# Loading the second FFN weight in two halves behind the first key transfers

## The chip, the cores and the metric

The kernel runs on one core of a Trainium2 chip. The core has five engines, each of which works through its own list of instructions in order: PE (TensorE, matrix products into PSUM banks; its weight loads are shown apart, as PEld), DVE (VectorE), ACT (ScalarE), POOL (GpSimd) and SP (SyncE). Here SP does nothing but issue DMA transfers. They all go into one queue, which 16 DMA engines work off. An instruction can wait for a semaphore that another engine, or a landed transfer, has raised. While it waits, everything behind it on its own engine waits too. The metric is the device time of one execution in microseconds (us). The figure for the kernel before is the median of three runs.

## The reference

A transformer block with attention and a gated feed-forward network (FFN) side by side, both fed from the same normalized input:

```
xn = layernorm(x)                       # x: 1 x 2048 x 512, bf16
q, k, v = split(xn @ wqkv)              # 32 heads of 16
p = softmax(q @ k.T * 16 ** -0.5)       # per head, 2048 x 2048
attn = (p @ v) @ wo
h = silu(xn @ w1) * (xn @ w3)           # 2048 x 1792
out = x + attn + h @ w2                 # w2: 1792 x 512
```

## The kernel before

**Scheduling.** The Python code of `_build` does not write the engines' lists out by hand. It keeps queues of work items (`miscq`, `expq`, `redq`, `poolq`, `spq` and others) and in a loop (L2034) takes, over all engines, the item that could start first by its own model of durations. So the order on each engine is fixed when the program is built. The item goes to the end of its engine's list together with the waits that its data need. Transfers enter `spq` through `later_dma`; an item with a `pred` is a candidate only once that function returns true. Among the candidates `pick_sp` (L2015) takes the one that could start earliest. On the chip SP then issues strictly in the order so found. Each transfer raises one of 24 semaphores, used in rotation.

**Start.** The input x and the weight wqkv are loaded (L596, L600), then two tiles of x again and the first pieces of w1 and w3 (L996, L624, L626), and two DRAM buffers are filled with constants (L614, L617). x is normalized in 16 tiles of 128 rows. PE transposes each (L771), and ACT copies the transposed tile t out as `xnT` tile t (L778); the name ("xnT", t) then enters the set `done`.

**Keys and queries.** Heads go in groups of four, and within a group each head takes a 32-row strip of the partitions. For the first group PE writes keys and queries straight into that layout. For the others ACT copies a product into `kq` (L857), a transfer spreads it into a DRAM buffer (kd or qd, L828), and a second one fetches it back as `KT` or `QT` in the strip layout (L845, L850). The first such key transfers are the pair KT<-kd at 21.14 us in the trace.

**Attention.** Work goes by units: one group of heads and 256 query rows (a few units have 128). In a first pass PE computes all scores of a unit (L1166) and DVE takes the maximum of each row (L1205). The negated maxima go into spare rows of `QT`: for the first units through PE and ACT (L922), for the others through a transposing transfer `Zs<-Z` (L1353) and two copies `QT<-Zs` (L1349). In a second pass PE computes the scores again, transposed and with the maximum taken off, and ACT takes the exponential into `PT` (L1479, or L1509 over two banks). PE then multiplies `PT` by the values `Vaug` (L673).

**Masked queries.** The second pass has two forms for a block of scores. One uses the 32-row strip of a single head (L1454). The other uses all 128 rows of `KT` against `BD`, which holds the unit's queries with the strips of the other three heads at zero (L669). `bd_prep` puts four transfers `BD<-QT` on `spq` for each unit, one for each head (L1291). Each copies 32 rows, for a unit of 128 query rows 8 KB in all. Where the built program uses `BD`, PE's matmul waits for that transfer.

**FFN and output.** w1 and w3 come in pieces of 128 columns, 128 KB each, as the work proceeds (L624, L626). `w2` is loaded once. `wo` is cleared by POOL (L652), and when that has been put on POOL's list, `late_loads` puts the four transfers of `wo` (L657, 128 KB each, into 16 of the 128 partitions) and the one of `w2` (L659, 1,792 KB, all 128 partitions, rows of 1 KB) on `spq`. The transfer of `w2` has no `pred` and waits for no data. `g_h` is the matmul that reads `w2`; it first runs at 349.3 us.

Of the kernel before, what the change touches and what calls it, by code (L numbers as in the profile page):

```python
# [254 lines left out]
def _c_mm(n):  # L255
    return n / 2400.0 + (0.007 if n >= 512 else 0.004)
# [6 lines left out]
def _build(nc, A_x, A_wqkv, A_wo, B_w1, B_w3, B_w2, out):  # L263
# [5 lines left out]
    FC = F // 128  # L269
# [40 lines left out]
    BD_END = 4  # L310
    NORM = "dddppppp"
    STATS = "dddddaaa"
    R_STAT = 2
    R_SEC = 1
    SPLIT_LO = 20
# [137 lines left out]
    def sb(name, shape, dt):  # L453
        return ctx.enter_context(nc.sbuf_tensor(name, list(shape), dt))

    with ctx:
# [7 lines left out]
        xnT = sb("xnT", [128, DC, S], BF16)  # L464
        hT = sb("hT", [128, NHT, 512], BF16)
# [14 lines left out]
        w2 = sb("w2", [128, FC, D], BF16)  # L480
# [46 lines left out]
        w2_v = B_w2.rearrange("(c p) n -> p c n", p=128)  # L527
# [19 lines left out]
        done = set()  # L547
# [12 lines left out]
        def later_dma(fn, reads, writes, lat=2.3, cb=None, pred=None, occ=0.62):  # L560
            spq.append(_Item(fn, reads, writes, occ, lat, cb, pred))
# [50 lines left out]
        def prefill():  # L612
            for b_ in range(2):
                later_dma(lambda e, b_=b_: e.dma_start(  # L614
                    kd[b_][:, 16:32, :], ones_t[:, :].unsqueeze(1).broadcast_to([128, 4, 128])),
                    [("ones_t",)], [("kd", b_)], lat=4.0, cb=lambda op, b_=b_: kd_free["K"].append(b_))
                later_dma(lambda e, b_=b_: e.dma_start(qd[b_][:, 16:32, :], Z[:, :, :, :]),  # L617
                          [("Z", 0), ("Z", 1)], [("qd", b_)], lat=4.0,
                          cb=lambda op, b_=b_: kd_free["Q"].append(b_))

        def load_w13(idx):
            fc = idx % FC
            sl = idx % 3
            later_dma(lambda e: e.dma_start(w13[:, sl, 0:DC, :], w1_v[:, :, fc * 128:(fc + 1) * 128]),  # L624
                      [], [("w13", sl, 0)])
            later_dma(lambda e: e.dma_start(w13[:, sl, DC:2 * DC, :], w3_v[:, :, fc * 128:(fc + 1) * 128]),  # L626
                      [], [("w13", sl, 1)], cb=lambda op: done.add(("w13", idx)))
# [13 lines left out]
        for g in padq:  # L641
# [7 lines left out]
                                  pred=lambda: ("AUG", 0) in done))  # L649
        poolq["pad"].append(_Item(lambda e: e.memset(Vaug[:, :, :, 16:17], 1.0), [],  # L650
                                  [("Vone",)], 2.4, pred=lambda: ("AUG", 0) in done))
        poolq["pad"].append(_Item(lambda e: e.memset(wo[:, :, :], 0.0), [], [("wo",)], 3.5,  # L652
                                  cb=lambda op: late_loads(), pred=lambda: ("AUG", 1) in done))

        def late_loads():
            for j in range(4):
                later_dma(lambda e, j=j: e.dma_start(wo[32 * j:32 * j + 16, :, :], wo_v[j]), [("wo",)],  # L657
                          [("wor", j)])
            later_dma(lambda e: e.dma_start(w2[:, :, :], w2_v), [], [("w2",)], lat=12.0)  # L659


        def col_groups(bk, make_lhsT, rhs_ap, ncols, c0=0, start=True, stop=True, m=32, skip=False, n=4, own=False):
            full = n == 4 and m == 32 and not own

            def part(a, b, start, skip):
                def f(e):
                    kw = dict(skip_group_check=True) if skip else {}
                    if full:
                        return e.matmul(bank(bk)[:, c0 + a:c0 + b], make_lhsT(0, 128), rhs_ap(0)[:, a:b],  # L669
                                        start=start, stop=stop, **kw)  # L670
                    for i in range(n):
                        rhs = rhs_ap(i)
                        ins = e.matmul(bank(bk)[32 * i:32 * i + m, c0 + a:c0 + b], make_lhsT(i),  # L673
                                       rhs if (a, b) == (0, ncols) else rhs[:, a:b],
                                       start=start, stop=stop, tile_position=(0, 32 * i), **kw)
                    return ins
                f.full = full
                return f
            f = part(0, ncols, start, skip or ncols == 512)
            if ncols == 512:  # L680
                f.piece = lambda a, b: part(a, b, start and a == 0, True)
                f.at = 0
            return f
# [3 lines left out]
        def ln_chunk(gi):  # L687
# [4 lines left out]
            left = [t1 - t0]  # L692
            on_act = STATS[gi] == "a"
            if on_act:
# [234 lines left out]
        def hslot(idx):  # L929
            return (idx + DC) % NHT  # L930
# [73 lines left out]
        def g_h(tg, fc, stop=False):  # L1004
            qc, ts = divmod(tg, 4)
            hs = hslot(qc * FC + fc)
            return (lambda bk: col_groups(bk, lambda i, z=32: hT[:, hs, ts * 128 + 32 * i:ts * 128 + 32 * i + z],
                                          lambda i: w2[:, fc, :], D, start=False, stop=stop),
                    [("hT", hs), ("w2",)], _c_mm(512), None)

        def g_on(qc, ts, g, start, stop):
            ob = (qc + 1) % 2
# [9 lines left out]
        def tile_OUT(tg):  # L1022
            qc, ts = divmod(tg, 4)
            groups = [g_x(tg)] + [g_h(tg, fc) for fc in range(FC)]
            groups += [g_on(qc, ts, g, False, g == NG - 1) for g in range(NG)]

            def evac(bk):
                def cb(op):
                    store(tg)
                    done.add(("OUT", tg))  # L1030
                    if tg + NXR < NT:
                        load_xr(tg + NXR)
                return [_Item(lambda e: e.activation(osb[:, tg % 4, :], bank(bk), ACTF.Identity),
                              [("ps", bk)], [("osb", tg % 4)], _c_act(512), cb=cb)]
            return _Tile("OUT%d" % tg, groups, evac, pred=lambda: ("xr", tg) in done
                         and (tg < 4 or ("ST", tg - 4) in done)
                         and all(("hT", qc * FC + fc) in done for fc in range(FC))
                         and all(("ON", qc, g, ts) in done for g in range(NG)), paced=True)
# [4 lines left out]
        def tile_OUTA(tg):  # L1043
            qc, ts = divmod(tg, 4)
            groups = [g_x(tg)] + [g_h(tg, fc, NGA == 0 and fc == FC - 1) for fc in range(FC)]
            groups += [g_on(qc, ts, g, False, g == NGA - 1) for g in range(NGA)]

            def evac(bk):
                def cb(op):
                    done.add(("OUTA", tg))  # L1050
                    if tg + NXR < NT:
                        load_xr(tg + NXR)
                if to_dve():
                    return [_Item(lambda e: e.tensor_scalar(opart[ts], bank(bk), 1.0, 0.0, ALU.mult, ALU.add),
                                  [("ps", bk)], OP_KEYS[ts], _c_dve(512), cb=cb, name="dve")]
                return [_Item(lambda e: e.activation(opart[ts], bank(bk), ACTF.Identity),
                              [("ps", bk)], OP_KEYS[ts], _c_act(512), cb=cb)]
            return _Tile("OUTA%d" % tg, groups, evac, pred=lambda: ("xr", tg) in done
                         and all(("hT", qc * FC + fc) in done for fc in range(FC))
                         and all(("ON", qc, g, ts) in done for g in range(NGA)))  # L1060
# [869 lines left out]
        def cand(eng, it, dma=False):  # L1930
            return max(P.free[eng], P.ready(eng, it.reads, it.writes, dma))
# [13 lines left out]
        def pick_act():  # L1945
# [13 lines left out]
            for k, it in enumerate(miscq[:14]):  # L1959
                if okp(it):  # L1960
                    s = cand("act", it)
                    r = {"first": 0, "second": R_SEC, "stat": R_STAT}.get(it.name, 2)
                    if m is None or s < m[0] - 1e-6 or (s < m[0] + 1e-6 and r < m[2]):
# [65 lines left out]
        load_w13(0)  # L2029
        load_w13(1)  # L2030
        prefill()

        seg = [0]
        while True:  # L2034
# [49 lines left out]
def bass_parallel_sum__mha_block__glu_gated_swiglu__prompt_kernel(  # L2084
    nc: bass.Bass,
    A_x: bass.AP,
    A_wqkv: bass.AP,
    A_wo: bass.AP,
    B_x: bass.AP,
    B_w1: bass.AP,  # L2090
    B_w3: bass.AP,
    B_w2: bass.AP,
    out: bass.AP,
):
    _build(nc, A_x, A_wqkv, A_wo, B_w1, B_w3, B_w2, out)
# [28 lines left out]
```

## Time and profile before

| | us |
|---|---|
| median of three runs | 1195.73 |
| the three runs | 1195.73, 1195.26, 1197.73 |
| the profiled execution | 1194.81 |
| its span, first to last instruction | 1193.1 |
| DVE busy in it | 1167.4 |
| ACT busy in it | 1164.2 |
| PE busy in it | 1113.7 |
| POOL busy in it | 460.7 |
| mean granted clock of PE | 0.995 of full speed |

The profile is of one execution. A row of the timeline gives the start, the duration, the engine, the source line, the operation, what it writes and reads (out<-in), how many were merged, and in brackets the idle time before it with what ended it. SPq rows are the issues of transfers on SP, not the transfers themselves. Buffer numbers are left out of names, so `w` stands for `w2` and for the pieces of w1 and w3 alike; the line tells them apart. A row "A <- B: total, times, longest" of the waits says that A sat idle until B was done. The chain follows the last instruction back through what released it at each step.

### The profile page before, as it was taken

Reading aid. Unit: us, or ns where it says so; the run is one execution under the profiler, and the core shown is the slowest. Engines: PE = TensorE matmul, PEld = TensorE weight load, DVE = VectorE, ACT = ScalarE, POOL = GpSimd, SP = SyncE. Lnnn points to the kernel's source line nnn. Section 1 sums busy time; section 2 is a strip of 40 time slices with the busy share of each in tenths; the row PEclk is TensorE's granted clock in tenths of the full one; section 3 lists DMA queues with packets and bytes.
Section 4 is the critical chain, followed back from the end, with each engine's and each line's share of the span. In section 5 each row is a group of like instructions: output and inputs, shape, how many; then the busy total and the mean of one; then the engine's idle time right before and its main releaser. Section 6 shows DMA issues by size and latency. Waiting matters only on the chain.

```text
span 1193.1 us, 36078 instructions
## 1 busy us (share of the span) xinstructions
PE 1113.7 (93%) x14891; PEld 527.2 (44%) x15026; DVE 1167.4 (98%) x1083; ACT 1164.2 (98%) x2259; POOL 460.7 (39%) x925
## 2 busy tenths in 40 slices
PE   8799999989999999999989999999999999989998
PEld 4344444334444443444434443444434444345654
DVE  8799999999999999999999999999999999999995
ACT  7699999999999999999999999999999999999998
POOL 5334473334433236343342135534342125533320
PEclk9899999999999999999999999999999999999999
DMA  5412323211101112211111112111110112101100
GB/s 181 125 47 71 92 55 80 58 40 45 42 22 40 42 45 53 51 31 36 32 39 29 43 44 63 40 41 33 44 27 22 42 33 62 28 23 22 25 20 23
DMA packets 144040, 56.34 MB, mean 47 GB/s; under 512 B 105996, under 2 KB 143876, under 8 KB 143876
## 3 DMA queue, kind: packets, MB, share of 16 engines
q1 hardware_dynamic: 143876, 54.02, 17.8%
q8 instruction: 119, 1.95, 0.7%
q14 instruction: 45, 0.37, 0.1%
HBM read 38.67 MB, written 6.74 MB: 38 GB/s over the span
## 4 chain that ended last, share of the span: by engine, by line
ACT 66%; PE 20%; DVE 12%; issue 1%; DMA 1%; POOL 0%; ACTq 0%; SPq 0%; POOLq 0%
ACT PT L1479 46%; DVE part L1205 11%; ACT PT L1509 10%; PE ps L669 8%; PE ps L673 4%; PE ps L1454 4%; PE ps L1166 4%; ACT zg L968 2%; ACT th L962 2%; ACT ub L972 2%; ACT U L1573 1%; DMA BD<-QT 1%; ACT kq L857 1%; ACT RB L1273 1%; PE ps L1815 1%
## 5 line engine op out<-in xcount | busy, mean ns | idle before, releaser
L1205 DVE TENSOR_REDUCE part<-ps 128x2 f32<-128x1024 f32 x1004 | 1138.4, 1211 | 8.4 <-PE ps L1454 7.4
L1479 ACT ACTIVATE PT<-ps 128x512 bf16<-128x512 f32 x1720 | 928.5, 750 | 8.8 <-PE ps L669 6.3
L1454 PE MATMUL ps<-QT,KT 32*128 32x256 bf16 (+1 forms) x3322 | 447.8, 257 | 10.4 <-ACT PT L1509 1.5
L1166 PE MATMUL ps<-KT,QT 32*128 32x512 bf16 x2066 | 419.4, 384 | 11.6 <-DVE part L1205 7.6
L1454 PEld LDWEIGHTS ps<-QT,KT 32*128 32x128 bf16 x3322 | 157.3, 92 | 159.0 <-ACT PT L1479 79.1
L673 PE MATMUL ps<-PT,Vaug 128*17 128x256 bf16 (+1 forms) x4672 | 205.0, 261 | 2.3 <-ACT PT L1479 0.2
L1509 ACT ACTIVATE PT<-ps 128x1024 bf16<-128x1024 f32 x164 | 187.8, 1177 | 0.7 <-PE ps L1454 0.6
L1166 PEld LDWEIGHTS ps<-KT,QT 32*128 32x128 bf16 x2066 | 102.8, 91 | 159.6 <-DVE part L1205 86.5
L1598 POOL TENSOR_TENSOR Rc<-Lc,mone 128x8 f32<-128x8 f32 (+1 forms) x69 | 105.0, 1522 | 158.2 <-DMA Lc<-U 157.9
L669 PE MATMUL ps<-xnT,w 128*128 128x512 bf16 (+3 forms) x606 | 151.7, 313 | 13.1 <-ACT PT L1479 4.2
L669 PE MATMUL ps<-BD,KT 128*128 128x256 bf16 (+1 forms) x834 | 147.4, 266 | 13.8 <-DMA BD<-QT 6.2
L673 PEld LDWEIGHTS ps<-PT,Vaug 128*17 128x17 bf16 x4672 | 91.7, 90 | 77.9 <-issue 56.4
L673 PE MATMUL ps<-BD,KT 128*32 128x256 bf16 (+1 forms) x2064 | 93.6, 265 | 0.3 <-ACT kq L857 0.2
L669 PEld LDWEIGHTS ps<-BD,KT 128*128 128x128 bf16 x834 | 64.8, 98 | 50.3 <-ACT PT L1479 11.1
L669 PEld LDWEIGHTS ps<-xnT,w 128*128 128x128 bf16 x647 | 50.4, 97 | 76.7 <-issue 36.6
L669 PE MATMUL ps<-w,hT 128*128 128x512 bf16 (+3 forms) x332 | 78.1, 304 | 4.1 <-ACT U L1573 2.6
L1330 POOL TENSOR_TENSOR mx<-part 128x16 f32<-128x16 f32 (+1 forms) x67 | 14.1, 211 | 169.3 <-DVE part L1205 169.0
L669 PE MATMUL ps<-xnT,ident 128*128 128x512 bf16 (+3 forms) x238 | 67.3, 318 | 12.4 <-DVE part L1205 4.9
L951 POOL TENSOR_TENSOR hT<-a,t 128x512 bf16<-128x512 f32 x56 | 71.0, 1268 | 2.9
L949 POOL TENSOR_TENSOR a<-zg,ub 128x512 f32<-128x512 bf16 x56 | 64.6, 1153 | 19.5 <-ACT ub L972 19.5
L1618 POOL TENSOR_TENSOR wk_on<-U,R 128x256 bf16<-128x256 f32 (+1 forms) x36 | 22.9, 636 | 119.6 <-DMA R<-rd 119.5
L947 POOL TENSOR_SCALAR t<-th 128x512 f32<-128x512 bf16 x56 | 34.7, 620 | 85.8 <-ACT th L962 84.9
(110 smaller groups left out, 746.9 us busy)
## 6 DMA issues: line engine op xcount, KB each, us to landing
w<-in_B_w_dram SPq DMA_DIRECT2D x112, 128.0 KB
R<-rd SPq DMA_DIRECT2D x55, 128.0 KB
QT<-qd SPq DMA_DIRECT2D x31, 128.0 KB
KT<-kd SPq DMA_DIRECT2D x28, 128.0 KB
BD<-QT SPq DMA_DIRECT2D x220, 16.0 KB
PT<-in_A_x_dram SPq DMA_DIRECT2D x4, 512.0 KB
xr<-in_A_x_dram SPq DMA_DIRECT2D x16, 128.0 KB
out_dram<-osb SPq DMA_DIRECT2D x16, 128.0 KB
```

The lines of the kernel that those rows point to most:

```text
L669: return e.matmul(bank(bk)[:, c0 + a:c0 + b], make_lhsT(0, 128), rhs_ap(0)[:, a:b], start=start, stop=stop, **kw)
L673: ins = e.matmul(bank(bk)[32 * i:32 * i + m, c0 + a:c0 + b], make_lhsT(i), rhs if (a, b) == (0, ncols) else rhs[:, a:b], start=start, stop ...
L947: q.append(_Item(lambda e: e.tensor_scalar(t1[:, :], th[:, ss, :], 1.0, 1.0, ALU.mult, ALU.add), [("th", ss)], [("t1",)], 0.62, 0.72))
L949: q.append(_Item(lambda e: e.tensor_tensor(a32[:, :], zg[:, ss, :], ub[:, ss, :], ALU.mult), [("zg", ss), ("ub", ss)], [("a32",)], 1.1, 1.25))
L951: q.append(_Item(lambda e: e.tensor_tensor(hT[:, hslot(idx), :], a32[:, :], t1[:, :], ALU.mult), [("a32",), ("t1",)], [("hT", hslot(idx))] ...
L962: lazyq.append(_Item(lambda e: e.activation(th[:, ss, :], zg[:, ss, :], ACTF.Tanh), [("zg", ss)], [("th", ss)], 0.52, cb=part_done))
L1166: ins = e.matmul(bank(2 * sl + i), QT[32 * j:32 * j + 32, qs, q * 128:(q + 1) * 128], KT[32 * j:32 * j + 32, g, c_ * 512:(c_ + 1) * 512], ...
L1205: redq.append(_Item(lambda e: e.tensor_reduce(dst, pair_ap.rearrange("p (a b) -> p a b", b=512), AX.X, ALU.max), writes, [("part", par, qt ...
L1454: ins = e.matmul(bank(b)[:, i * nq:(i + 1) * nq], KT[32 * j:32 * j + 32, g, (k0 + i) * 128:(k0 + i + 1) * 128], QT[32 * j:32 * j + 32, qs, ...
L1479: expq.append(_Item(lambda e: e.activation(PT[:, sl, :], bank(b), ACTF.Exp, scale=SCALE), [("ps", b)], [("PT", sl)], _c_act(512), cb=cb, e ...
L1509: return _Item(lambda e: e.activation(PT[:, s0:s1 + 1:s1 - s0, :], ps8[:, b0:b1 + 1:b1 - b0, :], ACTF.Exp, scale=SCALE), [("ps", b0), ("ps ...
L1598: poolq["nrm"].append(_Item(lambda e: e.tensor_tensor(Rc[:, pp, 0:nl], Lc[:, pp, 0:nl], mone[:, 0:nl], ALU.pow), [("Lc", pp), ("mone",)], ...
```

## The change

The transfer of `w2` leaves `late_loads`. In its place two transfers, of 7 of the 14 row blocks each, are put on `spq` right after the initial loads. Each may be taken once the scheduler has placed the copy of `xnT` tile 8, and each waits for that copy on the chip as well. `w2` now has two names, ("w2", 0) and ("w2", 1), and every matmul of `g_h` depends on both.

```
+    W2_AT = 8
...
             for j in range(4):
                 later_dma(lambda e, j=j: e.dma_start(wo[32 * j:32 * j + 16, :, :], wo_v[j]), [("wo",)],
                           [("wor", j)])
-            later_dma(lambda e: e.dma_start(w2[:, :, :], w2_v), [], [("w2",)], lat=12.0)
...
-                    [("hT", hs), ("w2",)], _c_mm(512), None)
+                    [("hT", hs), ("w2", 0), ("w2", 1)], _c_mm(512), None)
...
         prefill()
+        for i in range(0, FC, FC // 2):
+            later_dma(lambda e, i=i: e.dma_start(w2[:, i:i + FC // 2, :], w2_v[:, i:i + FC // 2, :]), [("xnT", W2_AT)],
+                      [("w2", i // (FC // 2))], lat=6.0, pred=lambda: ("xnT", W2_AT) in done)
```

In the built program the two halves stand on SP between the first KT<-kd pair and the qd<-kq that follows it, where before they stood, as one, between a kd<-kq and the second group of BD<-QT issues:

```
before                              after
KT<-kd x2                           KT<-kd x2
                                    w2<-B_w2 (7 of 14) x2
qd<-kq                              qd<-kq
QT<-qd x2                           QT<-qd x2
kd<-kq                              kd<-kq
KT<-kd x2                           KT<-kd x2
BD<-QT x4                           BD<-QT x4
kd<-kq                              kd<-kq
w2<-B_w2 (14 of 14)
BD<-QT x2                           BD<-QT x2
KT<-kd x2                           KT<-kd x2
BD<-QT x2                           BD<-QT x2
wo<-A_wo x4                         wo<-A_wo x4
```

The rest of SP's list, and the lists of PE, DVE, ACT and POOL, hold the same instructions in the same order. Some waits name another semaphore of the rotation, and four matmuls gain or lose a wait for a transfer that the other version has covered by an earlier one.

## The prediction

> **What bounds the kernel now.** I read the page's first part, then the busy time by stage, then the waits, the chain and the DMA queue of the one stage that falls out of line.
>
> ```profile
> span 1193.1 us, 36078 instructions
> PE 1113.7 (93%) x14891; PEld 527.2 (44%) x15026; DVE 1167.4 (98%) x1083; ACT 1164.2 (98%) x2259; POOL 460.7 (39%) x925
> ```
>
> DVE and ACT are both busy 98% of the span, so there are only some 26 and 29 us of idle time in which anything could be won without removing work. The busy time by stage says where they lie (columns: stretch, its length, busy us of PE, PEld, DVE, ACT, POOL, granted clock, DMA share, GB/s):
>
> ```profile
> 41.00:51.00 10.00, 9.50 (x111) 5.32 (x111) 9.94 (x11) 10.00 (x22) 6.56 (x6) 1.00 0.35 98
> 51.00:57.30 6.30, 0.08 (x1) 0.01 (x1) 1.12 (x1) 0.61 (x2) 1.65 (x8) 0.60 1.12 280
> 57.30:66.00 8.70, 8.05 (x72) 3.65 (x75) 6.40 (x6) 6.99 (x11) 0.00 (x0) 0.70 0.19 21
> 66.00:100.00 34.00, 33.07 (x488) 15.36 (x490) 34.00 (x31) 34.00 (x69) 13.82 (x27) 1.00 0.25 62
> 100.00:600.00 500.00, 470.27 (x5916) 213.09 (x5971) 499.71 (x446) 498.29 (x962) 207.59 (x381) 1.00 0.20 49
> 600.00:1100.00 500.00, 470.71 (x6274) 218.46 (x6325) 500.00 (x449) 498.80 (x971) 190.36 (x395) 1.00 0.15 37
> ```
>
> From 66 to 1100 us DVE is idle for 0.29 us in all and ACT for 2.9 us. Nothing is to be won there, and whatever moves the start of that stretch moves its end by as much. The hole is 51 to 66 us: in these 15 us DVE works 1.12 + 6.40 = 7.52 us and ACT 0.61 + 6.99 = 7.60 us, which leaves 7.48 and 7.40 us idle. The longest waits between 40 and 70 us say on what:
>
> ```profile
> DVE part L1205 <- PE ps L1454: 7.2, 3, 6.6
> ACT PT L1479 <- PE ps L669: 6.3, 1, 6.3
> PE ps L669 <- DMA BD<-QT: 6.2, 1, 6.2
> ```
>
> DVE and ACT wait for PE, and PE for one transfer, a masked-query copy BD<-QT. The chain in order of time gives that copy's life:
>
> ```profile
> 47.70 0.34 SPq L1291
> 48.05 0.04 issue
> 48.09 9.09 DMA BD<-QT
> 57.18 0.14 issue
> 57.32 0.80 PE ps L669 x5
> ```
>
> It is an 8 KB copy, and it took 9.09 us. The DMA queue's own rows say what stood ahead of it (start, length of the issue, line, out<-in, count):
>
> ```profile
> 21.14 0.82 SPq L845 DMA_DIRECT2D KT<-kd  x2
> 28.57 0.60 SPq L828 DMA_DIRECT2D qd<-kq  x1
> 31.45 0.80 SPq L850 DMA_DIRECT2D QT<-qd  x2
> ...
> 41.70 2.52 SPq L1291 DMA_DIRECT2D BD<-QT  x4
> 46.08 0.64 SPq L828 DMA_DIRECT2D kd<-kq  x1
> 46.76 0.45 SPq L659 DMA_DIRECT2D w<-in_B_w_dram  x1
> 47.31 1.71 SPq L1291 DMA_DIRECT2D BD<-QT  x2
> 49.22 0.90 SPq L845 DMA_DIRECT2D KT<-kd  x2
> 50.16 1.15 SPq L1291 DMA_DIRECT2D BD<-QT  x2
> 51.36 2.83 SPq L657 DMA_DIRECT2D wo<-in_A_wo_dram  x4
> 54.23 1.30 SPq L1353 DMA_TRANSPOSE Zs<-Z  x1
> 64.35 0.66 SPq L828 DMA_DIRECT2D kd<-kq  x1
> 65.06 1.13 SPq L1349 DMA_DIRECT2D QT<-Zs  x2
> ```
>
> The w<-in_B_w_dram at 46.76 is w2, all 1,792 KB of it, issued 0.55 us before the two copies on which PE then stops. So the stall is one small transfer behind one large one.
>
> **The change part by part.** In the order of instructions, PE, DVE, ACT and POOL run exactly what they ran before, in the same order; only SP's list differs.
>
> *w2 removed from 46.76.* PE stopped at 57.32 - 6.24 = 51.08 us. How late will the copy be without w2? Its two issues took 1.71 us, against 2.52 / 4 = 0.63 us each for the four at 41.70. They start at 47.3 in either case, since the first waits for ACT. So they end between 48.6 and 49.0. The nearest row for the landing of a transfer with nothing ahead of it is qd<-kq: its issue ends at 29.17, and what waits for it goes out at 31.45, 2.3 us later. BD then lands at 50.9 to 51.3, against 51.08 when PE wants it: a wait of 0 to 0.2 us. A copy of 8 KB should land sooner than one of 128 KB, so I take 0 and keep 0.3 us for the range. What goes with the wait is the slow clock behind it. The clock column gives its edges: 0.60 over 6.3 us means full speed up to 52.3, half after; 0.70 over the next 8.7 us means half speed until 62.5. So PE ran at half speed for 5.2 us after it had its data, and ACT's idle time beyond its 6.3 us wait, 7.40 - 6.3 = 1.1 us, is the price of that. With no pause neither occurs. Off this comes what a stretch of that length idles anyway: 0.06 us in ten before it for DVE, none for ACT. Both engines gain 7.4 us, and both are full up to 1100 us, so the end moves by 7.4 us less at most 0.3.
>
> *w2 put behind the first KT pair, in two halves.* The first half waits for ACT's copy of the ninth transposed tile, the L778 row that starts at 21.68:
>
> ```profile
> 21.68 0.63 ACT L778 ACTIVATE xnT<-ps 128x512 bf16<-128x512 bf16 x1
> ```
>
> It ends at 22.31, after the KT issues (21.14 + 0.82 = 21.96). SP's next instruction, qd<-kq, does not go out before 28.57, because it waits for ACT. So two issues of 0.45 us (w2's own row) fit, and nothing on SP stands behind the new wait. What the queue carries there (same columns as above):
>
> ```profile
> 3.00:13.00 10.00, 10.00 (x85) 7.59 (x82) 8.19 (x24) 3.65 (x10) 2.96 (x7) 1.00 1.09 371
> ...
> 24.00:29.00 5.00, 4.72 (x36) 1.94 (x35) 5.00 (x6) 5.00 (x15) 3.07 (x8) 1.00 0.00 0
> ...
> 55.00:58.00 3.00, 0.68 (x5) 0.46 (x5) 0.00 (x0) 0.06 (x1) 0.00 (x0) 0.50 1.15 121
> 58.00:60.00 2.00, 1.67 (x18) 0.83 (x18) 1.23 (x1) 1.95 (x3) 0.00 (x0) 0.50 0.34 39
> 60.00:62.00 2.00, 2.00 (x17) 0.61 (x14) 1.50 (x2) 1.35 (x3) 0.00 (x0) 0.50 0.00 1
> ```
>
> From 24 to 29 us it moves nothing. At the 371 GB/s of the opening loads, 1.835 MB take 4.9 us; at the slowest pace of a full queue in these rows, 121 GB/s, 15.2 us. The same kind of load (many rows of 1 KB over all partitions) gave the 371, so I take 4.9 us from the end of the two issues, 22.3 + 0.9 = 23.2: done at 28.1, at 30.4 with the 2.3 us of a landing, so qd<-kq is late by 0 to 1 us. The cover is in SP's waits:
>
> ```profile
> SPq L217 <- ACT QT L922: 5.2, 1, 5.2
> ```
>
> That is the first BD<-QT at 41.70, which stands behind qd, QT, kd and KT on SP and waited 5.2 us for ACT. Up to 5.2 us of delay reaches no engine. Cost taken: 0.
>
> *What is late next.* With BD on time, PE goes on through its list to the first scores that read the rows from Zs:
>
> ```profile
> 68.40 0.28 PE L1454 MATMUL ps<-QT,KT 32*128 32x256 bf16 x1
> ```
>
> That is 11.08 us after 57.32, of which 1.1 us was slow clock, so about 51.1 + 10.0 = 61.1 us. Their rows need the Zs transposition (54.23), and it stands behind wo. In the 121 GB/s of 55 to 58 us I read wo, 512 KB into 16 partitions a piece: 4.3 us at that pace, from about 52.4, so Zs lands near 57.5. QT<-Zs stands behind kd on SP, which follows ACT: 64.35 was 7.0 us after 57.32, so it comes at 51.1 + 5.9 = 57.0, and QT<-Zs at 57.7. Slack about zero in front of the issue, and then 65.06 to 68.40, 3.3 us from issue to use, of which some 2 are transfer. Cost 0, at worst the second rival below.
>
> *Sum.* The profiled execution took 1194.81 us around a span of 1193.1; 1194.81 - 7.4 = 1187.4. Its time lies 0.92 us under the median of the runs, 1195.73; on the median the forecast is **1188.3 us**. Its own range is 1187.2 to 1189.3: the 0.3 us above, 0.1 us more gain from DVE, and the rest for a median that scatters about 0.7 us.
>
> **The rivals.** *Zs takes the place of BD.* If wo is as slow without w2 beside it, the queue empties at 60 as it does now (39 GB/s up to 60, 1 after). Then QT<-Zs goes out at 60.0 to 61.1 and lands some 2 us later, 1 to 2 us after 61.1; say 1.5. The half clock came 1.2 us after PE had stopped (52.3 against 51.08), so it may come again and cost its 1.1 us: 1.5 to 2.6 us given back, 1189.8 to 1190.9. For it: wo's row at 121 GB/s. Against: SP issues it in the same place as before and has 512 KB to move, not 2.3 MB. The Trainium skill, TensorE: Matmul & The Clock Gate, Part 1, puts the fall to half clock after an idle window of about 3.4 us; by it this rival would cost 1.5 us alone, while this trace had the fall at 1.2 us.
>
> *BD is late all the same.* PE was released at 57.2, while w2 at 371 GB/s from about 48 should have ended near 53. If wo, not w2, held the copy (121 GB/s through 58 us speaks for that), PE waits until wo ends, 52.4 + 4.3 = 56.7: 0.6 us gained, 1195.1. Against: wo was issued at 51.36, 2.3 us after the copies; without w2 they should be gone by then.
>
> *Slower: w2 holds the queue in its new place.* Everything up to the first BD stands behind it on SP. Past 5.2 us of delay each us stalls PE, with 1.1 us of clock on top. It breaks even at 7.4 - 1.1 + 5.2 = 11.5 us, and at 13.9 us the kernel is 2.4 us slower, 1198.1. For this w2 would have to hold the queue from 23.2 until about 1 us before 31.45 + 13.9, so to 44: some 21 us, or 87 GB/s. Even at 121 GB/s it ends at 38.4, qd<-kq is some 8 us late and 4 of the 7.4 us go. Only a pace below all full-queue rows here makes it slower.
>
> **How the numbers follow.** Forecast 0.75; Zs 0.12; BD late all the same 0.08; w2 in the way 0.05. The range 1186.8 to 1191.4 takes in the forecast and the Zs case, and leaves out the last two. A measurement of this kernel tells 0.2%, 2.4 us, from no change: faster is 0.87 (the first two), same 0.08, slower 0.05.
>
> **What would show it.** Right: no wait of PE for BD<-QT in the waits, DVE busy above 9.9 us in 51 to 61, granted clock 1.00 through 51 to 66, a full queue between 24 and 29 us, BD<-QT at 41.70 unmoved. A PE wait for QT<-Zs near 61 means the second case; the BD wait still there, ending with wo, the third; a first BD<-QT later than 41.7 the fourth. I am wrong altogether if DVE shows new idle time between 66 and 1100 us.

## The result, and the profile after

| | kernel before | changed kernel |
|---|---|---|
| median, us | 1197.34 | 1190.53 |
| lowest to highest of six runs each | 1195.26 to 1200.19 | 1186.05 to 1194.20 |
| the profiled execution, us | 1194.81 | 1189.0 |
| its span, us | 1193.1 | 1187.3 |

The ratio of the times is 0.9944, with an interval of 0.9916 to 0.9972: 6.7 us less (3.4 to 10.1). Executions more than 1.5% above the fastest of their kernel (one of the kernel before took 1538.67 us, at a granted clock of 0.553) are left out of all medians and comparisons here.

The first part of the changed kernel's page:

```profile
span 1187.3 us, 36082 instructions
...
PE 1112.7 (94%) x14891; PEld 527.6 (44%) x15026; DVE 1167.6 (98%) x1083; ACT 1164.1 (98%) x2259; POOL 460.0 (39%) x925
```

DVE and ACT do the work that they did before (1167.4 and 1164.2 us), so all that was won is idle time. Where it went is in the busy time by stage, in the same stretches and columns as in the prediction (stretch, its length, busy us of PE, PEld, DVE, ACT, POOL with the counts, granted clock, DMA share, GB/s):

```profile
41.00:51.00 10.00, 9.42 (x109) 5.35 (x106) 9.95 (x11) 10.00 (x21) 6.44 (x7) 1.00 0.15 42
51.00:57.30 6.30, 5.83 (x70) 2.72 (x68) 6.30 (x7) 6.30 (x12) 1.28 (x6) 1.00 0.72 102
57.30:66.00 8.70, 8.28 (x218) 4.70 (x218) 8.70 (x9) 8.70 (x20) 0.41 (x1) 1.00 0.26 68
66.00:100.00 34.00, 32.58 (x353) 13.92 (x357) 33.68 (x31) 33.88 (x64) 20.08 (x34) 1.00 0.27 65
100.00:600.00 500.00, 469.36 (x5888) 212.42 (x5939) 499.28 (x446) 497.71 (x960) 204.75 (x380) 1.00 0.19 48
600.00:1100.00 500.00, 470.64 (x6358) 220.59 (x6410) 498.77 (x448) 497.40 (x969) 187.26 (x394) 0.99 0.15 37
```

The hole is gone. From 51 to 66 us DVE and ACT are busy throughout (6.30 + 8.70), where 7.48 and 7.40 us were idle, and the clock is 1.00 instead of 0.60 and 0.70. But DVE's idle time from 66 to 1100 us rose from 0.29 us to 0.32 + 0.72 + 1.23 = 2.27 us. The spans differ by 1193.1 - 1187.3 = 5.8 us: 7.5 from the hole, 0.5 from a start that happened to run earlier (the KT<-kd pair at 20.68 instead of 21.14, with w2 not yet issued), less the 2.0 given back there and 0.2 by which DVE's own work took longer. Most of the 2.0 lies in one place (same columns):

```profile
1055.00:1060.00 5.00, 5.00 (x109) 3.05 (x108) 3.81 (x4) 3.88 (x7) 3.21 (x9) 0.50 0.07 12
```

PE ran at half clock here and DVE lost 1.19 us. Whether that belongs to the change is a question for the runs below.

SP's own rows (start, length of the issue, line, out<-in, count) show the two halves and what comes behind them:

```profile
20.68 0.82 SPq L845 DMA_DIRECT2D KT<-kd  x2
21.86 0.99 SPq L2033 DMA_DIRECT2D w<-in_B_w_dram  x2
28.10 0.59 SPq L828 DMA_DIRECT2D qd<-kq  x1
30.91 0.81 SPq L850 DMA_DIRECT2D QT<-qd  x2
...
41.23 2.52 SPq L1291 DMA_DIRECT2D BD<-QT  x4
...
57.70 1.13 SPq L1349 DMA_DIRECT2D QT<-Zs  x2
```

Everything up to the first BD<-QT stands 0.46 to 0.54 us earlier than before (28.57, 31.45 and 41.70), like the pair of KT<-kd ahead of w2: nothing behind w2 was held up. The queue meanwhile, in the same columns as the stages:

```profile
24.00:29.00 5.00, 4.72 (x33) 1.70 (x30) 5.00 (x5) 5.00 (x14) 3.13 (x8) 1.00 0.99 345
55.00:58.00 3.00, 2.69 (x33) 1.33 (x34) 3.00 (x4) 3.00 (x7) 0.00 (x0) 1.00 0.65 66
58.00:60.00 2.00, 2.00 (x55) 1.19 (x54) 2.00 (x3) 2.00 (x5) 0.00 (x0) 1.00 0.12 39
```

It is full from 24 to 29 us (0.99, at 345 GB/s), where it moved nothing before. What SP still waits for, of its waits between 20 and 70 us:

```profile
SPq L217 <- ACT QT L922: 5.1, 1, 5.1
...
SPq L1349 <- DMA Zs<-Z: 0.9, 1, 0.9
```

The first is the cushion in front of the first BD<-QT, about as long as before (5.2). The second says that the transposition Zs<-Z landed at about 57.6 us. PE has no wait for BD<-QT and none for QT<-Zs between 40 and 70 us.

### The profile page after: what moved, and what is told of

The parts are those of the page before. It is cut to its first block, busy times and chain, and to the rows that moved or that the text cites. A ratio compares the mean times of both kernels' runs of the same rounds, so it can differ in the third digit from the quotient of the medians.

```text
span 1187.3 us, 36082 instructions
## 1 busy us (share of the span) xinstructions
PE 1112.7 (94%) x14891; PEld 527.6 (44%) x15026; DVE 1167.6 (98%) x1083; ACT 1164.1 (98%) x2259; POOL 460.0 (39%) x925
## 4 chain that ended last, share of the span: by engine, by line
ACT 61%; DVE 19%; PE 17%; issue 1%; DMA 1%; POOL 1%; SPq 0%; ACTq 0%; POOLq 0%
ACT PT L1479 43%; DVE part L1205 18%; ACT PT L1509 10%; PE ps L669 6%; PE ps L673 4%; PE ps L1454 3%; PE ps L1166 3%; ACT th L962 2%; ACT zg L968 2%; ACT ub L972 1%; ACT U L1573 1%; ACT kq L857 1%; ACT RB L1273 1%; PE ps L1815 1%; ACT xnT L778 1%
```

## The experiments

The theory: 7.4 us are won because the copies BD<-QT no longer stand behind w2, and the new place costs nothing. Its rivals: the new place helps in some other way, the halving does it, `wo` rather than `w2` held the copies, or the new time rests on chance in the clock. Each edit is against the kernel that its text names.

### Both kernels once more

The kernel before, unchanged:

> The kernel before, unchanged, for its spread and the granted clock of each run. Clock theory (a run that falls to half clock late in the span loses about 1.4 us for each such fall of some 7 us, whichever kernel runs): the runs lie within 1195 to 1201 us, those with the lowest mean clock are the longest, and the shortest has the profile's 0.995 or a little less. Rival (the change itself brings the late falls of the clock): all runs of this kernel show 0.995 and lie within 1.5 us of each other.

1198.21 us over 12 runs; ratio to the other runs of the same kernel 1.0011 [0.9992, 1.0029]. The waits of PE between 40 and 70 us again show 6.2 us for BD<-QT. But late in this execution stands a second such wait:

```profile
PE ps L669 <- DMA BD<-QT: 3.0, 1, 3.0
```

That is from its waits of PE between 1130 and 1160 us. And its clock falls near 1060 us, at the same point of the work where the changed kernel's fell near 1055 (same columns as the stages):

```profile
600.00:1100.00 500.00, 480.43 (x6296) 218.65 (x6291) 497.55 (x446) 496.38 (x965) 187.70 (x390) 0.99 0.15 37
1060.00:1065.00 5.00, 5.00 (x101) 3.31 (x99) 4.07 (x4) 3.90 (x7) 3.04 (x8) 0.56 0.06 13
1065.00:1070.00 5.00, 5.00 (x71) 2.92 (x68) 4.02 (x4) 4.13 (x9) 0.21 (x1) 0.50 0.13 34
```

DVE is idle for 2.45 us from 600 to 1100 us, and 1.91 of them lie in these 10 us. So late waits for a small copy, and late stretches of half clock, occur without the change too.

The changed kernel, unchanged:

> The changed kernel, unchanged, for the same reading and for a second trace. Queue theory (w2 held the masked-query copy back, nothing else): no PE wait for BD<-QT, DVE idle under 0.2 us in 41 to 66 us, 6 to 9 us below the kernel before. Clock theory: runs at clock 0.999 or 1.0 take about 1186 us, those near 0.993 about 1193. If the small DVE waits near 84 and 217 us (0.35 and 0.5 us in the first trace) belong to the new order, they stand in this trace too; if they are chance they are elsewhere or gone.

1189.48 us over 6 runs, ratio 0.9936 [0.9915, 0.9957]: 7.7 us less. The stages of this execution:

```profile
51.00:57.30 6.30, 5.70 (x63) 2.62 (x63) 6.18 (x6) 6.11 (x11) 1.54 (x8) 1.00 0.81 117
57.30:66.00 8.70, 8.52 (x224) 4.73 (x223) 8.70 (x9) 8.70 (x19) 0.35 (x1) 1.00 0.25 66
66.00:100.00 34.00, 33.38 (x353) 14.02 (x355) 33.88 (x30) 33.99 (x66) 19.75 (x34) 1.00 0.27 65
100.00:600.00 500.00, 478.80 (x5960) 212.60 (x5954) 499.75 (x447) 498.81 (x961) 205.91 (x381) 1.00 0.19 48
600.00:1100.00 500.00, 479.74 (x6475) 220.72 (x6473) 500.00 (x449) 498.81 (x974) 187.57 (x395) 1.00 0.15 37
```

DVE is idle from 66 to 1100 us for 0.12 + 0.25 = 0.37 us, and its small waits near 84 and 217 us are gone. The 2.0 us that the first execution gave back there are not the change's. This one lost its time later, as a row of PE's timeline shows (idle time before it in brackets):

```profile
1133.88 0.38 PE L669 MATMUL ps<-BD,KT 128*128 128x128 bf16 x4 [2.70 <-DMA BD<-QT]
```

Of the four BD<-QT issues just before, by the view of that line's instructions, one took 2.17 us instead of 0.58:

```profile
L1291 SPq DMA_DIRECT2D BD<-QT x4: 577/582/2166, 1129.3 to 1132.8; - x4
```

(shortest, middle, longest in ns). What held that issue is not known, and it need not be the cause. In the kernel before, the late wait of 3.0 us stands in front of the same four matmuls, and so do these two, of the run with one piece and of the run with two loads below:

```profile
1134.47 0.38 PE L669 MATMUL ps<-BD,KT 128*128 128x128 bf16 x4 [3.24 <-DMA BD<-QT]
1135.53 0.38 PE L669 MATMUL ps<-BD,KT 128*128 128x128 bf16 x4 [1.96 <-DMA BD<-QT]
```

In these three executions the four issues took 2.47 or 2.48 us together, 0.6 us each. So this wait belongs to a place that both kernels have, and comes in some executions and not in others; why the copy lands late there stays open.

### One piece or two halves

The changed kernel, with one transfer in the new place:

```
-for i in range(0, FC, FC // 2):
-    later_dma(lambda e, i=i: e.dma_start(w2[:, i:i + FC // 2, :], ...), [("xnT", W2_AT)], ...)
+later_dma(lambda e: e.dma_start(w2[:, :, :], w2_v), [("xnT", W2_AT)], [("w2", 0), ("w2", 1)],
+          lat=12.0, pred=lambda: ("xnT", W2_AT) in done)
```

> w2 in the new place but as one transfer. Queue theory: the place does it all, so the same as the changed kernel within 0.2% (2.4 us), no PE wait for BD<-QT, qd<-kq issued at the same time and QT<-qd within 0.5 us of the changed kernel's. Rival (two halves let small transfers in between, one piece does not): QT<-qd some 2 us later; still no stall of an engine, since 5 us of SP's wait cover it.

1191.22 us over 12 runs, ratio 0.9940 [0.9917, 0.9962]. Its hole is closed as well, but for 0.3 us:

```profile
51.00:57.30 6.30, 5.99 (x72) 2.71 (x71) 6.00 (x6) 6.03 (x10) 1.11 (x6) 1.00 0.75 107
```

The place matters, the halving does not, as far as this can be measured.

### w2 out of the way, but later

The kernel before, with w2 held back until ("AUG", 6) is in `done`:

```
-later_dma(lambda e: e.dma_start(w2[:, :, :], w2_v), [], [("w2",)], lat=12.0)
+later_dma(lambda e: e.dma_start(w2[:, :, :], w2_v), [], [("w2",)], lat=12.0,
+          pred=lambda: ("AUG", 6) in done)
```

> w2 in one piece, put far behind the start (after the sixth unit's masks), with only the old place emptied. Queue theory: the old stall is gone as in the changed kernel, 6 to 9 us below the kernel before; w2 may hold up a later small transfer by some 5 us, which costs 0 to 3 us there. Rival (the new place helps by itself, by moving w2 into idle queue time): clearly slower than the changed kernel, with a stall of 3 us or more at the new place.

1197.89 us over 11 runs, ratio 0.9993 [0.9971, 1.0016]: nothing won. The old hole is closed (DVE is busy for 6.30 of 6.30 us in 51 to 57.3). The timeline of SP and PE shows a new one:

```profile
138.56 0.45 SPq L659 DMA_DIRECT2D w<-in_B_w_dram  x1
139.62 2.49 SPq L1291 DMA_DIRECT2D BD<-QT  x4
...
146.30 0.58 PE L669 MATMUL ps<-BD,KT 128*128 128x256 bf16 x2 [2.17 <-DMA BD<-QT]
```

w2 again goes out right ahead of a group of BD<-QT, and PE again waits, 2.17 us. What that costs is in the stretches behind it:

```profile
145.00:150.00 5.00, 3.69 (x18) 1.10 (x19) 2.30 (x3) 2.30 (x4) 2.65 (x6) 0.59 0.41 97
150.00:155.00 5.00, 5.00 (x22) 1.24 (x20) 3.12 (x3) 2.97 (x5) 2.75 (x5) 0.50 0.27 65
155.00:160.00 5.00, 5.00 (x26) 1.10 (x22) 3.67 (x3) 3.67 (x6) 1.90 (x3) 0.50 0.21 53
160.00:165.00 5.00, 5.00 (x28) 1.31 (x27) 3.41 (x3) 3.82 (x8) 3.03 (x3) 0.71 0.23 53
```

The clock column gives 4.1 + 5 + 5 + 2.9 = 17.0 us at half speed, and DVE is idle for 2.70 + 1.88 + 1.33 + 1.59 = 7.5 of these 20 us: in this execution (1199.57 us) a wait of 2.17 us cost as much as the old one of 6.24. It does not always: two of the runs took 1190.23 and 1191.76 us, at clocks of 0.998 and 0.995. My expectation of a gain of several us was wrong, and the rival came true: it is not enough that w2 leaves its old place, the queue must be idle where it goes.

### w2 just behind the copies

The kernel before, with w2 held back until the second group of copies is issued, which puts it behind `wo` and in front of Zs:

```
+          pred=lambda: ("BD", 1, 1) in done)
```

> w2 in one piece behind the four copies and wo, just ahead of Zs: the prediction's second rival made to happen. Queue theory: no PE wait for BD<-QT, but Zs lands only when wo and w2 are through, 4.3 + 4.9 us after about 52.5, so near 62; QT<-Zs goes out at 62 and lands at 64, against a reader due at 60: a PE wait of 3 to 5 us for QT<-Zs, and the half clock with it, so 0 to 3 us faster than the kernel before. Rival (behind the copies nothing is urgent): as fast as the changed kernel.

1198.10 us over 9 runs, ratio 0.9997 [0.9982, 1.0013]. The waits of PE between 40 and 70 us:

```profile
PE ps L1454 <- DMA QT<-Zs: 4.4, 1, 4.4
...
PE ps L669 <- DMA BD<-QT: 0.3, 1, 0.3
```

SP's rows:

```profile
53.52 0.43 SPq L659 DMA_DIRECT2D w<-in_B_w_dram  x1
...
62.60 1.11 SPq L1349 DMA_DIRECT2D QT<-Zs  x2
```

The wait moved from one small transfer to the next, as expected. QT<-Zs goes out at 62.60 instead of 57.70 us. By the stages DVE is idle for 0.16 + 4.79 + 2.08 = 7.0 us from 51 to 100 us, beside 7.48 before.

### How much of the wait was wo's

The kernel before, with the four transfers of `wo` held back by `pred=lambda: ("AUG", 6) in done` (some later instructions shift with them):

> The kernel before with w2 where it was and the four wo transfers put off until the sixth unit. Is the 9 us of the masked-query copy due to w2 alone? Queue theory with w2 alone: wo is issued behind the copy and cannot hold it, so PE still waits about 6.2 us, until about 57. Rival (wo's slow transfer into 16 partitions, side by side with w2's tail, holds the copy): w2's 1.8 MB at 371 GB/s end near 53, the copy lands at 53 to 54 and PE waits 2 to 3 us.

One run, 1195.78 us. The wait of PE for BD<-QT between 40 and 70 us:

```profile
PE ps L669 <- DMA BD<-QT: 4.6, 1, 4.6
```

The queue with w2 alone in it:

```profile
53.00:54.00 1.00, 0.00 (x0) 0.00 (x0) 0.00 (x0) 0.00 (x0) 0.00 (x0) 0.79 0.94 310
54.00:55.00 1.00, 0.00 (x0) 0.03 (x1) 0.00 (x0) 0.00 (x0) 0.00 (x0) 0.50 0.40 97
```

w2 is through by about 54.5 us, and the copies land with it. The result lies between both theories: by these single executions, w2 alone makes 4.6 of the 6.2 us, and `wo` beside it the other 1.6.

### Two halves around the old place

The kernel before, with w2 as two transfers, the first where w2 stood:

```
-later_dma(lambda e: e.dma_start(w2[:, :, :], w2_v), [], [("w2",)], lat=12.0)
+for i in range(0, FC, FC // 2):
+    later_dma(lambda e, i=i: e.dma_start(w2[:, i:i + FC // 2, :], w2_v[:, i:i + FC // 2, :]), [],
+              [("w2", i // (FC // 2))], lat=12.0)
...
```

The second half then follows `wo`.

> The old place, but w2 in two halves: the scheduler puts the first where w2 stood and the second behind wo, ahead of Zs. Place theory: half the bytes ahead of the copy, so a PE wait for BD<-QT of 0 to 2 us instead of 6.2, and a new wait for QT<-Zs near 60 us of 1 to 4 us, because Zs stands behind wo and the second half; with the clock's share 0 to 5 us of the 7.4 us are gained. Rival (the two halves do it, not the place): no wait in either, as fast as the changed kernel.

1195.32 us over 10 runs, ratio 0.9967 [0.9943, 0.9991]. PE's wait for the copies is halved (lines stand two lower in this kernel):

```profile
PE ps L671 <- DMA BD<-QT: 2.3, 1, 2.3
```

The stall that I expected at QT<-Zs was 0.3 us, probably because the half clock behind the 2.3 us (0.70 and 0.63 of full speed in 51 to 57.3 and 57.3 to 66 us) made PE come to those rows later. By the ratio, half of w2 in the way leaves 1 to 7 us of gain, with 4 us, about half, in the middle; the profiled execution (1196.26 us) still has DVE idle for 2.97 + 2.58 = 5.6 us in these 15 us, beside 7.48 before.

### How much room the new place has

The changed kernel with w2 loaded once more, and twice more, right behind the two halves, into rows of PT and hT that nobody uses yet:

```
+later_dma(lambda e: e.dma_start(PT[:, NT:NT + FC, :], w2_v), [("xnT", W2_AT)],
+          [("PT", NT + i) for i in range(FC)], lat=6.0, pred=lambda: ("xnT", W2_AT) in done)
```

Once more:

> The changed kernel with one more load of w2 in the new place (w2 in its two halves, then once more whole, into rows of PT that are not in use yet; its result is read by nobody). The question is how much of the cushion in front of the first BD<-QT one load uses. Theory of the prediction: two loads are 3.67 MB, 9.9 us of a full queue at 371 GB/s from 23.2, so the queue is full until about 33; qd<-kq and QT<-qd come 2 to 5 us late (QT<-qd at 33 to 36 instead of 30.9), the first BD<-QT stays within 1 us of 41.2, because up to 5.1 us of delay disappears in SP's wait for ACT, PE waits less than 0.5 us for BD<-QT and DVE stays above 9.9 us in 51 to 61. The time is that of the changed kernel, 1186 to 1194. Rival: already the second load uses up the room in the queue, SP is held in an issue for several us as with three loads, the first BD<-QT moves by 2 us or more and PE stalls: then one load is near the limit as well.

One run, 1191.54 us. Its rows on SP:

```profile
21.25 0.82 SPq L845 DMA_DIRECT2D KT<-kd  x2
...
28.68 0.59 SPq L828 DMA_DIRECT2D qd<-kq  x1
36.38 0.81 SPq L850 DMA_DIRECT2D QT<-qd  x2
...
41.81 2.52 SPq L1291 DMA_DIRECT2D BD<-QT  x4
```

The execution started 0.57 us later (KT<-kd at 21.25). With that taken off, qd<-kq goes out on time (28.68), though it was expected 2 to 5 us late as well; it is its landing that is late, since QT<-qd behind it is 36.38 - 30.91 - 0.57 = 4.9 us late. The first BD<-QT is not late at all. PE has no wait for BD<-QT, and DVE is full from 51 to 66 us.

Twice more:

> The changed kernel with two more loads of w2 behind the two halves (into buffers not yet in use): three times the bytes in the new place, 5.5 MB, 14.8 us at 371 GB/s, done near 38 to 39. By the prediction's sum for its slower rival: qd<-kq lands some 8 us late, QT, kd and KT follow, the 5.1 us of SP's wait for ACT are used up, the first BD<-QT goes out about 3 us late and PE waits 0 to 3 us for it at 47, with the half clock behind. Rival (the queue lets small transfers through): QT<-qd and the first BD<-QT within 0.5 us of the changed kernel's.

One run, 1198.5 us. Its rows on SP:

```profile
23.76 5.83 SPq L2037 DMA_DIRECT2D hT<-in_B_w_dram  x1
29.69 4.67 SPq L828 DMA_DIRECT2D qd<-kq  x1
41.66 0.82 SPq L850 DMA_DIRECT2D QT<-qd  x2
...
46.21 2.53 SPq L1291 DMA_DIRECT2D BD<-QT  x4
```

The third load and qd<-kq took 5.83 and 4.67 us to issue. QT<-qd is 10.5 us late (the start 0.26 us later taken off), the first BD<-QT 4.7, and PE waits 2.7 us; expected were some 8, about 3, and 0 to 3. So a delay of 4.9 us disappears in the cushion, and of 10.5 us all but 5.8 comes through: the cushion is some 5 us, as read from SP's wait.

### A try for a version that beats both

In the changed kernel, more of the matmuls that only keep PE busy, from entry 105 of the scheduler's list of settings (`TUNE`) on, against the late half clock:

```
+if seg[0] > 104:
+    K.HEAT_FILL = max(K.HEAT_FILL, 3.0)
+    K.HEAT_P1 = max(K.HEAT_P1, 1.5)
```

> A try for a version that beats both: the changed kernel, with more of the matmuls that only keep PE busy (some 116 more rows on PE) in the units after number 104 of the list, where stretches of half clock of 3 to 10 us were seen near 1055 and 1135 us after PE had waited 2 to 3 us for a copy or had little to do. Theory: the run-to-run scatter comes from such stretches, so they become rarer: mean granted clock 0.998 to 1.000 in most runs, the median 1186 to 1188, 1.5 to 3 us under that of the changed kernel's runs (1189.5 to 1190.5). Rival: the added matmuls stand in front of scores on PE and hold ACT or DVE up by as much as the steadier clock brings, or the clock falls after waits that no matmul fills: the clock's spread stays 0.992 to 1.000 and the median 1189 to 1193.

1192.53 us over 7 runs (1191.15 to 1193.25), ratio 0.9945 [0.9921, 0.9969]. The clock did what I hoped, 0.999 or 1.000 in all seven runs. The time did not: at a clock of 1.000 it is 1191.15 and 1191.84 us, where the changed kernel has 1186.05 and 1186.22. So by two runs of each the added matmuls cost some 5 us themselves.

The second form, with `HEAT_FILL` at 2.0, `HEAT_WIDE` at 1.4 and `BD_NEAR` at 0.1 in its place:

> A second form of the same try: fewer added matmuls, and over a wider time around each gap, in the units after number 104. Theory: as in e10, with less in the way: mean granted clock 0.997 to 1.000, median 1186 to 1189. Rival: no steadier clock than the changed kernel has (0.992 to 1.000), the median 1189 to 1192, the interval of the ratio to the kernel before overlaps that of the changed kernel (0.9915 to 0.9957).

1197.13 us over 12 runs, ratio 0.9991 [0.9967, 1.0015], clocks of 0.989 to 0.997: no steadier, and it loses the gain. In its profiled execution the hole is closed (DVE is busy for 6.30 and 8.70 us in the two stretches); the time goes at the end, where the clock is 0.86 from 1100 to 1187 us. None of the versions beats the changed kernel.

## Why the prediction was right

**The wait and its cause** stood as read: one small copy behind w2. Where "the stall is one small transfer behind one large one" falls short is its share: with `wo` away 4.6 of the 6.2 us stay, so about a quarter was `wo`'s (one execution each). The rival by which `wo` alone held the copy falls with the same run: 1.6 us, not 5.6.

**The size**, 7.4 us, is what the hole gave back. DVE has 7.48 us less idle time there in the first execution and 7.36 in the second (0.12 us are left). The two ratios give 6.7 and 7.7 us.

**The new place** cost nothing, by the steps given: a free stretch of SP from 22 to 28 us, a queue full between 24 and 29, qd<-kq and the first BD<-QT where they were. The cushion of 5.2 us, read off one wait, held when it was used on purpose. At twice the load the prediction's way of working it out (9.9 us at 371 GB/s) still gives the delay: 2 to 5 us expected for QT<-qd, 4.9 measured.

**What is late next.** QT<-Zs was put at 57.7 us and came at 57.70, but that it fits to the hundredth is luck. The prediction had it follow kd<-kq, put at 57.0; that went out at 56.01, and SP then waited 0.9 us for Zs<-Z, which was put near 57.5 and landed at about 57.6. The pace of `wo` was read about rightly: without w2 beside it, it is nearly as slow as the rival assumed (columns of the stages; 136 GB/s beside 121).

```profile
53.00:56.00 3.00, 2.92 (x34) 1.27 (x33) 3.00 (x3) 3.00 (x7) 0.00 (x0) 1.00 1.13 136
```

`wo` ended in time because nothing large stood ahead of it. PE reached the rows at 60.06 us, an us sooner than the 61.1 worked out (half of it the earlier start), and did not wait. The slack is thin: with w2 in front of Zs the issue came 4.9 us later and PE waited 4.4, so some 0.4 us were left.

**What was mis-sized is the clock.** The prediction took the half clock as a tail of the stall, at 1.1 us. In the hole this held, with 5.2 us at half speed after PE had its data. But "it may come again and cost its 1.1 us", the price for a second wait of 1.5 us, leaves out how long the half clock lasts. Behind the wait of 2.17 us it lasted 17.0 us, and the two cost 7.5 us of DVE's time; behind the late wait of 1.96 us there was none. Had Zs taken the place of BD, it could have taken back the whole gain, not a third.

**"I am wrong altogether if DVE shows new idle time between 66 and 1100 us"** was too hard a test. The first execution does show 2.0 us. The second does not, and the kernel before, run again, idles there for 0.09 + 2.45 = 2.5 us of its own, so such losses are not the change's. A single execution cannot pass or fail a test of 2 us when runs of one kernel lie 8 us apart.

**The scatter** was put at 0.7 us, by the three runs shown. Most of it goes with the clock: over the 24 runs with w2 in the new place, in one piece or two, the time falls by 1.0 us for each 0.001 of mean granted clock (correlation -0.81), and it reaches from 1185.76 us at 1.000 to 1195.05 at 0.994. The median of the kernel before is 1198.2 us over 29 runs, so the three runs at 1195.73 were low by 2.4 us. The forecast on that base was about as much too low: 1190.53 lies outside its own range of 1187.2 to 1189.3, and inside the wider one, which had its room from the Zs rival and not from the scatter. That the wider one held is partly luck.

## What to carry to other kernels

A stall of PE on a copy of 8 KB can be a matter of what stands ahead of it in the queue: look up the issue before it, and move that to where the DMA share is 0.00 and SP's next waits are long, not merely away. Price every place on the way by the small transfers behind it, since a big load put just behind the first victim finds the second. And where PE is close to the bound, a wait of 2 us can cost as much as one of 6, because of the half clock that may follow it; compare medians of many runs before reading 2 us of idle time as the work of a change.

## What the runs showed of the hardware

**The half clock comes in steps of 3.4 us.** A clock of 0.60 over 6.3 us means 2 x 0.40 x 6.3 = 5.0 us at half speed. Worked out so from the clock columns, its stretches last 3.4 us (behind the late 2.70 us wait of the changed kernel: 0.58, 0.50, 0.50 and 0.72 in the four us from 1134), 6.8 (near 1055 us: 0.94 and 0.65 in the us on both sides of six at 0.50; and in the hole of the kernel before in its second execution: 0.71 over 6.3 and 0.82 over 8.7 us), 10.2 (in its first: 0.60 and 0.70) and 17.0 (w2 late): one, two, three and five times 3.4. The Trainium skill, TensorE: Matmul & The Clock Gate, Part 1, gives a free-running window of about 3.4 us, and the lengths agree. The fall to half clock after an idle window of that length, as it gives it, does not: here it came 1.2 us after PE had stopped (51.08 to 52.3), and after waits of 2.17 and 2.70 us. Near 1055 us it came where PE had waited no longer than 0.7 us at a time, and the late wait of 1.96 us in the run with two loads brought none. What else decides whether a wait brings it, and how many steps it lasts, stays open.

**The queue took about two of these loads before SP stood.** In the new place, with one and two loads of w2 in it, issues took 0.4 to 0.6 us each; the third took 5.83 us and the 128 KB transfer behind it 4.67, so SP itself stands when the queue is full. What stands in it matters too: behind `wo` and a single w2 (w2 just behind the copies) the issue of Zs<-Z took 3.68 us instead of 1.30.
